# Attention, a mixture of experts and a soft mixture on one core: work on h's operands a step later, weight differences and dispatch at other places

## The chip, the cores and the metric

The kernel runs on one core of a Trainium2 chip. The metric is the device time of one execution in microseconds, the median of a few runs. TensorE multiplies matrices; its output goes to PSUM banks, which VectorE (DVE in the profile) and ScalarE (ACT) must empty before a bank can be used again. SyncE (SP) issues nearly all DMA transfers. GpSimd (POOL) has next to nothing to do.

## The reference

Three stages follow each other, for 2304 tokens of width 512:

```python
kv  = einsum('bhsd,bhse->bhde', k, v)            # attention, 4 batches of 576 tokens, 8 heads of 64
out = einsum('bhsd,bhde->bhse', q, kv)
x   = out / sqrt(mean(out*out, -1) + 1e-6) * g_norm
# mixture of experts, dense: every token goes through all 4 experts
for e in range(4):
    h = maximum(x @ w1[e], 0)                    # 512 -> 1024
    y += p[:, e:e+1] * (h @ w2[e])               # 1024 -> 512
# soft mixture: 8 experts x 4 slots, on y
logits = y @ phi                                 # 2304 x 32
d = exp(logits - logits.max(0)); d /= d.sum(0) + 1e-9     # dispatch: softmax over the tokens
slots = d.T @ y                                  # then a small two-layer network for each expert
c = softmax over the slots of logits
result = c @ slot_out
```

## The kernel before

**Tiles and chunks.** The 2304 tokens are 18 tiles of 128. Chunks 0 to 3 hold four tiles each, chunk 4 two. The first mixture goes through the chunks in two groups: group 0 is chunks 0 and 1, with experts 0, 1, 2, 3; group 1 is chunks 2, 3 and 4, with experts 3, 2, 1, 0. Expert 3 is thus used by both groups one after the other, and its weights stay in SBUF (it is the one called KEPT); those of experts 0 to 2 are prepared for group 0, stored to DRAM and read back for group 1.

**Products.** For accuracy each f32 operand is split into two f16 numbers, a high and a low half, and a product takes three f16 matmuls. The high half is a conversion on ScalarE (for weights L607, for h L821 and L823), the low half is the difference of the number and its high half, on VectorE (L609, L828, L832); the low half therefore waits for the high one. "First product" means h = relu(x w1), "second product" means h w2 with the addition to the output, scaled by p. Both are done for most chunks with seven block products in place of eight (numbered P 1 to 7), for which sums and differences of blocks of x, of h and of the weights are needed: S1 to S4 of h, T1 to T4 of a weight. In a first product TensorE writes to p (L913), and `fast_h` (L810) empties it with copies on ScalarE (L845, L847, L849, L863) and additions on VectorE (L851, L855, L859) and makes the operands of h. In a second product TensorE writes to m (L1012), and L1026 on ScalarE and L1028 on VectorE add m into the output; the second products of expert 3 for chunk 0, and of some others, take another form (y, L976, L987).

**The main list.** All of this is a list of 548 steps of TensorE's work, written out in order; a usual step takes 1.31 us, one of chunk 4's first product about half. Expert 3 runs through all chunks from step 180 to 314:

| steps | what | begins at, us |
|---|---|---|
| 180 to 193, 194 to 209 | chunk 0, first and second product | 281.4, 305.45 |
| 210 to 223 | chunk 1, first product | 328.82 |
| 224 to 237 | chunk 2, first product (group 1 begins) | 360.47 |
| 238 to 251 | chunk 1, second product | 385.58 |
| 252 to 265 | chunk 3, first product | 410.30 |
| 266 to 279 | chunk 2, second product | 437.31 |
| 280 to 293 | chunk 4, first product | 456.53 |
| 294 to 307, 308 to 314 | chunks 3 and 4, second product | 465.91, 484.25 |
| from 315 | expert 2 with group 1 | 493.42 |

**Background work.** Everything else is cut into small steps and strewn between the main ones: the preparing of weights, the attention of the next chunks (with its products kv, L278, o, L333, and xT, L402), and the dispatch softmax of finished chunks (`disp_steps`). `chain(start, stop, steps, ...)` (L1329) spreads such a list evenly from main step start to main step stop; `run_bg` takes from each chain what is due. So the place of an instruction in an engine's order follows from the marks given to its chain. An engine works through its order strictly; an instruction that waits holds up all behind it. `pe(f)` defers a background step's TensorE part until the main step's matmuls are issued.

The chains that the change touches: `prep_t2(e)` (L714) makes the differences T1 to T4 of expert e's w2 for group 1: in two halves four subtractions on VectorE (L727), four high parts on ScalarE (L607) and four low parts on VectorE (L609), and for e = 0 to 2 two stores each to DRAM. `kv_steps(3)` and `attn_steps([3])` are the attention of batch and chunk 3; kv's two banks are copied to kvs on VectorE (L302). `disp_steps(c)` computes chunk c's logits (lg, L1068), their maximum (L1088, L1092), the exponential dT (L1107, on ScalarE), its transpose dtr on TensorE (L1115) with the copy d (L1131), the product sp with its sum sacc (L1150), and the softmax over the slots (L1168 to L1186). ScalarE loads a table (ACT_TABLE_LOAD) when it passes between the square root of the attention (L377) and an exponential.

**Tasks on h.** The work on h's operands that isn't done at once is put in a queue, `todo`, as small tasks; `work_off(n, c, op)` (L804) takes n of them at each main step, and all up to the one for operand (c, op) before a product needs that:

```python
while todo and (n > 0 or any(o == (c, op) for o, _ in todo)):
    todo.popleft()[1]()
    n -= 1
```

**Loads.** SBUF is 47 pages of 4 KB in each partition, and PSUM eight banks. `want` puts loads in one list, and `pump` issues them in that order on SyncE's queue when pages are free, leaving as many free as the running chains claim. The read-backs of an expert's operands ("o1", "o2") stand at the end of the list, and the list halts at them until the main step gate[e]:

```python
key = loads[0][0]
if key[0] in ("o1", "o2") and now < gate[key[1]]:
    return
load_next()
```

## Time and profile before

| | us |
|---|---|
| median of 3 runs | 841.62 (841.59 to 842.0) |
| the profiled execution | 840.22 |
| its span, first to last instruction | 838.3 |
| TensorE busy | 806.4 (96%) |
| VectorE busy | 565.5 (67%) |
| ScalarE busy | 371.4 (44%) |

TensorE's granted clock was 0.997 of full speed in the mean. The busy shares are means over stages with different limits: in some stages VectorE has as much to do as TensorE, in others half of it. A row "[2.19 <-ACT pages L863]" says that the engine was idle for 2.19 us before this instruction, and that an instruction of ScalarE at line 863 that writes pages ended it.

### The profile page before, as it was taken

Reading aid. Unit: us, or ns where it says so; the run is one execution under the profiler, and the core shown is the slowest. Engines: PE = TensorE matmul, PEld = TensorE weight load, DVE = VectorE, ACT = ScalarE, POOL = GpSimd, SP = SyncE. Lnnn points to the kernel's source line nnn. Section 1 sums busy time; section 2 is a strip of 40 time slices with the busy share of each in tenths; the row PEclk is TensorE's granted clock in tenths of the full one; section 3 lists DMA queues with packets and bytes.
Section 4 is the critical chain, followed back from the end, with each engine's and each line's share of the span. In section 5 each row is a group of like instructions: output and inputs, shape, how many; then the busy total and the mean of one; then the engine's idle time right before and its main releaser. Section 6 shows DMA issues by size and latency. Waiting matters only on the chain.

```text
span 838.3 us, 17438 instructions
## 1 busy us (share of the span) xinstructions
PE 806.4 (96%) x7409; PEld 630.8 (75%) x7409; DVE 565.5 (67%) x1106; ACT 371.4 (44%) x735; POOL 13.1 (2%) x16
## 2 busy tenths in 40 slices
PE   7989999999999999889799999999999999999996
PEld 6865748575766676678689988898889888984444
DVE  7889978956895567778887426875488638742403
ACT  2684565653556145664565435240454125421202
POOL 4000000000000000000000000000000000000000
PEclk9999999999999999999999999999999999999998
DMA  8950700294239632100112350042202262669697
GB/s 331 387 216 26 248 4 21 91 380 188 76 102 405 247 114 113 51 27 1 51 52 74 105 180 23 1 177 98 105 2 93 89 223 76 214 235 355 197 402 232
DMA packets 40910, 126.01 MB, mean 150 GB/s; under 512 B 4224, under 2 KB 11264, under 8 KB 40832
## 3 DMA queue, kind: packets, MB, share of 16 engines
q1 hardware_dynamic: 40384, 124.80, 40.5%
q8 instruction: 58, 0.95, 0.5%
q14 instruction: 20, 0.16, 0.1%
q10 hardware_dynamic: 448, 0.10, 0.1%
HBM read 96.57 MB, written 28.31 MB: 149 GB/s over the span
## 4 chain that ended last, share of the span: by engine, by line
PE 80%; DVE 12%; ACT 5%; issue 1%; DMA 1%; ACTq 0%; DVEq 0%
PE p L913 31%; PE m L1012 20%; PE y L976 19%; PE s L1657 2%; PE so L1687 2%; PE kv L278 1%; PE o L333 1%; DVE mx_w L535 1%; DVE pages L930 1%; DVE pages L476 1%; DVE t L943 1%; DVE pages L609 1%; ACT pages L821 1%; DMA gT<-in_g 1%; PE x2T L1045 1%
## 5 line engine op out<-in xcount | busy, mean ns | idle before, releaser
L913 PE MATMUL p<-pages 128*128 128x256 f16 (+1 forms) x3360 | 340.9, 262 | 1.5 <-DVE pages L476 0.5
L913 PEld LDWEIGHTS <-pages 128*128 128x128 f16 x3360 | 299.9, 98 | 37.2 <-issue 5.1
L1012 PE MATMUL m<-pages 128*128 128x256 f16 x1680 | 186.5, 273 | 4.2 <-DVE pages L1028 4.2
L1012 PEld LDWEIGHTS <-pages 128*128 128x128 f16 x1680 | 164.1, 98 | 23.7 <-issue 4.9
L976 PE MATMUL y<-pages 128*128 128x512 f16 x768 | 170.9, 379 | 1.2 <-DVE pages L930 1.1
L976 PEld LDWEIGHTS <-pages 128*128 128x128 f16 x768 | 74.7, 98 | 87.0 <-DVE pages L930 1.6
L1028 DVE SCALAR_TENSOR_TENSOR pages<-m,pc,pages 128x256 f32<-128x256 f32 x120 | 53.6, 480 | 59.2 <-PE m L1012 59.0
L607 ACT ACTIVATE pages<-pages,s_w 128x512 f16<-128x512 f32 (+1 forms) x113 | 77.9, 739 | 32.3 <-DVE s_w L585 11.6
L609 DVE SCALAR_TENSOR_TENSOR pages<-pages,s_w 128x512 f16<-128x512 f32 (+1 forms) x113 | 83.9, 778 | 3.6 <-ACT pages L607 3.5
L823 ACT CAST pages<-t 128x512 f16<-128x512 f32 (+1 forms) x72 | 39.1, 549 | 65.8 <-DVE t L866 33.1
L929 ACT ACTIVATE pages<-t 128x512 f16<-128x512 f32 x48 | 30.0, 628 | 39.3 <-DVE t L943 38.9
L821 ACT ACTIVATE pages<-pages 128x512 f16<-128x512 f32 (+1 forms) x48 | 26.8, 558 | 46.1 <-DVE pages L855 24.5
L938 ACT COPY t<-p 128x512 f32<-128x512 f32 x48 | 27.1, 582 | 43.7 <-PE p L913 43.7
L943 DVE TENSOR_TENSOR t<-p,t 128x512 f32<-128x512 f32 x48 | 32.7, 686 | 17.2 <-PE p L913 17.1
L832 DVE TENSOR_TENSOR pages<-t,pages 128x512 f16<-128x512 f32 (+1 forms) x72 | 42.4, 596 | 2.3 <-ACT pages L823 0.9
L828 DVE SCALAR_TENSOR_TENSOR pages<-pages 128x512 f16<-128x512 f32 (+1 forms) x48 | 28.6, 599 | 15.4 <-ACT pages L821 15.0
L930 DVE SCALAR_TENSOR_TENSOR pages<-t,pages 128x512 f16<-128x512 f32 x48 | 32.8, 683 | 8.6 <-ACT pages L929 7.9
L987 DVE SCALAR_TENSOR_TENSOR pages<-y,pc,pages 128x512 f32<-128x512 f32 x24 | 18.0, 749 | 26.1 <-PE y L976 26.1
L823 ACT CAST pages<-pages 128x512 f16<-128x512 f32 (+1 forms) x24 | 13.0, 550 | 37.8 <-DVE t L870 37.8
L851 DVE TENSOR_TENSOR t<-p,t 128x512 f32<-128x512 f32 (+1 forms) x24 | 14.4, 598 | 19.4 <-PE p L913 16.6
L845 ACT COPY t<-p 128x512 f32<-128x512 f32 (+1 forms) x24 | 11.8, 515 | 31.2 <-PE p L913 31.1
L855 DVE TENSOR_TENSOR pages<-p,pages 128x512 f32<-128x512 f32 (+1 forms) x24 | 14.3, 598 | 16.4 <-PE p L913 14.8
(179 smaller groups left out, 705.3 us busy)
## 6 DMA issues: line engine op xcount, KB each, us to landing
pages<-in_w SPq DMA_DIRECT2D x48, 512.0 KB, 7.9
o<-pages SPq DMA_DIRECT2D x33, 512.0 KB, 9.8
pages<-o SPq DMA_DIRECT2D x33, 512.0 KB, 4.8
pages<-in_m SPq DMA_DIRECT2D x32, 512.0 KB, 5.2
pages<-in_m2a SPq DMA_DIRECT2D x16, 512.0 KB, 4.7
pages<-in_m2b SPq DMA_DIRECT2D x16, 512.0 KB, 10.3
o_t<-pages SPq DMA_DIRECT2D x12, 512.0 KB, 2.6
pages<-o_t SPq DMA_DIRECT2D x12, 512.0 KB, 4.5
```

Of the source, the lines that this page charges most:

```text
L607: nc.scalar.activation(dst[:, 0], src, AF.Copy, scale=s)
L609: nc.vector.scalar_tensor_tensor(out=dst[:, 1], in0=src, scalar=s, in1=dst[:, 0], op0=ALU.mult, op1=ALU.subtract)
L821: nc.scalar.activation(dst, sh(src), AF.Relu)
L823: nc.scalar.copy(dst, sh(src))
L832: nc.vector.tensor_tensor(out=h[:, 1], in0=sh(src), in1=h[:, 0], op=ALU.subtract)
L913: nc.tensor.matmul(ps[:, fp * n:fp * n + n], l, r, start=(fp + i == 0 and P in first), stop=(fp == 1 and i == len(mms) - 1 and P in end), ...
L929: nc.scalar.activation(hh, src, AF.Relu)
L930: late.append(lambda: nc.vector.scalar_tensor_tensor(out=hl, in0=src, scalar=0.0, in1=hh, op0=ALU.max, op1=ALU.subtract))
L943: nc.vector.tensor_tensor(out=t, in0=ps, in1=t, op=ALU.add)
L976: nc.tensor.matmul(ps, a, b, start=(u + kk + fp + i == 0), stop=(u == 1 and kk == 1 and fp == 1 and i == 2))
L1012: nc.tensor.matmul(ps, l, r, start=(i == 0 and j == 0 and P in (1, 2, 7)), stop=(i == len(mms) - 1 and j == nh - 1 and P in (2, 3, 4)), sk ...
L1028: nc.vector.scalar_tensor_tensor(out=x, in0=src, scalar=pc, in1=x, op0=ALU.mult, op1=ALU.add)
```

## The change

There are five edits.

1. A task that is put in `todo` may be taken not by the next call of `work_off` but from the one after it on: `turn` counts the calls, and each task carries its number. What a product needs is still taken ahead of that product.
2. Expert 2's `prep_t2` moves from steps 182 to 206 to steps 280 to 307 (from chunk 4's first product on). Its raw loads move behind the loads of q 6 to 8 and wait for step 274.
3. Expert 3's `prep_t2` moves from steps 208 to 225 to steps 194 to 223.
4. Dispatch of chunk 0 is spread over steps 210 to 237 in place of 210 to 223, that of chunk 1 over 255 to 279 in place of 252 to 265.
5. The attention of chunk 3 begins at step 222 in place of 224.

```diff
@@ pump
-            if key[0] in ("o1", "o2") and now < gate[key[1]]:
+            if now < gate.get(key[1] if key[0] in ("o1", "o2") else key[:3], now):
                 return
@@ the list of loads
-    want_t(E - 2)
     want_t(E - 1)
     want_kv(7)
     want_kv(8)
     for i in range(6, 9):
         want(("q", i), qT[i], 4)
+    want_t(E - 2)
@@ work_off
+        turn[0] += 1
-        while todo and (n > 0 or any(o == (c, op) for o, _ in todo)):
+        while todo and (n > 0 and todo[0][2] < turn[0] or any(o == (c, op) for o, _, _ in todo)):
             todo.popleft()[1]()
@@ fast_h
-            todo.append(((c, op), f))
+            todo.append(((c, op), f, turn[0] + 1))
@@ the chains
-    chain(m["mm1", 1, E - 1, 2], m["mm1", 1, E - 1, 3], kv_steps(3) + attn_steps([3], V), 6, 1.0)
+    chain(m["mm1", 1, E - 1, 2] - 2, m["mm1", 1, E - 1, 3], kv_steps(3) + attn_steps([3], V), 6, 1.0)
-    chain(m["mm1", 0, E - 1, 1], m["mm1", 1, E - 1, 2], disp_steps(0), 2, 1.0)
-    chain(m["end", 0, E - 1, 1], m["mm2", 1, E - 1, 2], disp_steps(1), 2, 1.0)
+    chain(m["mm1", 0, E - 1, 1], m["mm2", 0, E - 1, 1], disp_steps(0), 2, 1.0)
+    chain(m["end", 0, E - 1, 1] + 3, m["end", 1, E - 1, 2], disp_steps(1), 2, 1.0)
     for e in FAST:
-        chain(m["mm1", 0, e + 1, 0] + 2, m["mm1", 0, e + 1, 1] - (0 if e < E - 2 else 4), prep_t2(e, V), 4)
+        if e < E - 2:
+            chain(m["mm1", 0, e + 1, 0] + 2, m["mm1", 0, e + 1, 1], prep_t2(e, V), 4)
+        else:
+            chain(m["mm1", 1, E - 1, 4], m["mm2", 1, E - 1, 4], prep_t2(e, V), 4)
+            gate["w2", 1, e] = m["mm1", 1, E - 1, 4] - 6
         gate[e] = m["mm1", 1, e + 1, 3]
-    chain(m["mm1", 0, E - 1, 1] - 2, m["mm1", 1, E - 1, 2] + 2, prep_t2(E - 1, V), 4)
+    chain(m["mm2", 0, E - 1, 0], m["mm1", 1, E - 1, 2], prep_t2(E - 1, V), 4)
```

The lines of the new kernel have numbers two higher behind L806 (L828 is L830, L1028 is L1030, L913 is L915).

The orders below show three places. In the names, t_0_3_1_1 is the temporary of chunk 1's first product with expert 3, second half; p_0_3_2_0 and p_0_3_2_1 are the banks of chunk 2's first product; s_w_3 and s_w_2 are the scales of expert 3's and expert 2's weights; kv_3706 and kv_3605 are kv of batch 3.

First place: VectorE where chunk 2's first product begins (step 224), before:

```order
L609 SCALAR_TENSOR_TENSOR pages<-pages,s_w_3_2800 128x512
L832 TENSOR_TENSOR pages<-t_0_3_1_0_3382,pages 128x512
L609 SCALAR_TENSOR_TENSOR pages<-pages,s_w_3_2800 128x512
L832 TENSOR_TENSOR pages<-t_0_3_1_1_3406,pages 128x512
L851 TENSOR_TENSOR t_0_3_2_0_3730<-p_0_3_2_0_3770,t_0_3_2_0_3730 128x512
L870 SCALAR_TENSOR_TENSOR pages<-pages 128x512
L851 TENSOR_TENSOR t_0_3_2_1_3757<-p_0_3_2_1_3796,t_0_3_2_1_3757 128x512
L870 SCALAR_TENSOR_TENSOR pages<-pages 128x512
L302 COPY kvs<-kv_3706 64x4x64 x2
```

and now:

```order
L868 SCALAR_TENSOR_TENSOR t_0_3_1_0_3359<-t_0_3_1_0_3359,pages 128x512
L868 SCALAR_TENSOR_TENSOR t_0_3_1_1_3375<-t_0_3_1_1_3375,pages 128x512
L1170 TENSOR_REDUCE mc_3689<-ltr_3630 128x4
L1172 TENSOR_TENSOR ce_3691<-ltr_3630,mc_3689 128x128
L834 TENSOR_TENSOR pages<-t_0_3_1_0_3359,pages 128x512
L302 COPY kvs<-kv_3605 64x4x64 x2
L853 TENSOR_TENSOR t_0_3_2_0_3685<-p_0_3_2_0_3725,t_0_3_2_0_3685 128x512
L834 TENSOR_TENSOR pages<-t_0_3_1_1_3375,pages 128x512
```

Expert 3's low parts are gone from here, dispatch 0's softmax over the slots has come, and the copies of kv stand ahead of chunk 2's first additions rather than behind them. On TensorE the matmul that follows the last kv has, in the new order, a wait that the old one has not:

```order
L915 MATMUL p_0_3_2_0_3672<-pages 128x256
L278 MATMUL kv_3605<-pages 64x64 x10
L915 LDWEIGHTS pages [waits DVE_49]
L915 MATMUL p_0_3_2_1_3703<-pages 128x256 [waits PE_49]
L915 LDWEIGHTS pages
```

The wait is for VectorE's copies of kv, whose bank p_0_3_2_1 takes over.

Second place: VectorE in chunk 4's first product (steps 280 to 293), before:

```order
L832 TENSOR_TENSOR pages<-t_0_3_3_0_4289,pages 128x512
L832 TENSOR_TENSOR pages<-t_0_3_3_1_4313,pages 128x512
L851 TENSOR_TENSOR t_0_3_4_0_4844<-p_0_3_4_0_4862,t_0_3_4_0_4844 128x256
L828 SCALAR_TENSOR_TENSOR pages<-t_0_3_4_0_4844,pages 128x256
L851 TENSOR_TENSOR t_0_3_4_1_4860<-p_0_3_4_1_4878,t_0_3_4_1_4860 128x256
L828 SCALAR_TENSOR_TENSOR pages<-t_0_3_4_1_4860,pages 128x256
L855 TENSOR_TENSOR pages<-p_0_3_4_0_4831,pages 128x256
L828 SCALAR_TENSOR_TENSOR pages<-pages 128x256
```

and now:

```order
L834 TENSOR_TENSOR pages<-t_0_3_3_1_4268,pages 128x512
L727 TENSOR_TENSOR pages<-pages 128x2x256 x2
L853 TENSOR_TENSOR t_0_3_4_0_4808<-p_0_3_4_0_4828,t_0_3_4_0_4808 128x256
L727 TENSOR_TENSOR pages<-pages 128x2x256
L853 TENSOR_TENSOR t_0_3_4_1_4825<-p_0_3_4_1_4844,t_0_3_4_1_4825 128x256
L830 SCALAR_TENSOR_TENSOR pages<-t_0_3_4_0_4808,pages 128x256
L727 TENSOR_TENSOR pages<-pages 128x2x256
L830 SCALAR_TENSOR_TENSOR pages<-t_0_3_4_1_4825,pages 128x256
L609 SCALAR_TENSOR_TENSOR pages<-pages,s_w_2_2016 128x512 x2
L857 TENSOR_TENSOR pages<-p_0_3_4_0_4795,pages 128x256
L609 SCALAR_TENSOR_TENSOR pages<-pages,s_w_2_2016 128x512
L857 TENSOR_TENSOR pages<-p_0_3_4_1_4812,pages 128x256
```

Expert 2's subtractions and low parts have come between the additions, and a low half of h (L830) no longer stands right behind the addition it belongs to.

Third place: ScalarE where dispatch 1's exponential dT is computed, before:

```order
L847 COPY pages<-p_0_3_3_1_4300 128x512
L849 COPY pages<-p_0_3_3_0_4444 128x512
L377 ACTIVATE rms_4326<-rms_4326 128x16
L1107 ACT_TABLE_LOAD
L1107 ACTIVATE dT_4464,sm_4465<-LT_92,neg_4437 128x128
```

and now:

```order
L1028 ACTIVATE pages<-m_0_3_2_4510,pc_2805 128x256 x2
L408 COPY pages<-xT_4617 128x512
L1109 ACT_TABLE_LOAD
L1109 ACTIVATE dT_4639,sm_4640<-LT_92,neg_4572 128x128
L1111 ACTIVATE al_4577<-al_4577 128x1
```

It has moved from chunk 3's first product, where it stood among the copies from p, to chunk 2's second product, where it stands behind the emptying of m.

## Rows read from the trace of the kernel before

**Rows 1.** The page: TensorE's busy time, share and instructions

```profile
PE 806.4 (96%) x7409; PEld 630.8 (75%) x7409; DVE 565.5 (67%) x1106; ACT 371.4 (44%) x735; POOL 13.1 (2%) x16
```

**Rows 2.** TensorE's timeline, 318 to 496 us, all with idle time ahead (start, duration)

```profile
340.22 1.06 PE L1068 MATMUL lg<-pages,phiT 128*32 128x128 f32 x26 [0.40 <-ACT pages L1057]
...
350.63 0.33 PE L1115 MATMUL dtr<-ident,dT 128*128 128x128 f32 x1 [3.64 <-ACT dT L1107]
...
359.59 0.95 PE L278 MATMUL kv<-pages 64*64 64x64 f32 x20 [2.19 <-ACT pages L863]
...
395.45 2.78 PE L1012 MATMUL m<-pages 128*128 128x256 f16 x24 [0.98 <-DVE pages L1028]
...
400.71 5.40 PE L1012 MATMUL m<-pages 128*128 128x256 f16 x48 [1.60 <-DVE pages L1028]
...
407.69 2.78 PE L1012 MATMUL m<-pages 128*128 128x256 f16 x24 [1.58 <-DVE pages L1028]
...
413.89 0.44 PE L1045 MATMUL x2T<-ident,pages 128*128 128x128 f32 x2 [1.90 <-DVE pages L1028]
```

**Rows 3.** Busy time by stage: PE, PEld, DVE, ACT, POOL (instructions), clock, DMA

```profile
328.82:360.47 31.65, 25.39 (x257) 20.88 (x255) 24.15 (x47) 19.86 (x42) 0.00 (x0) 1.00 0.12 39
...
385.58:410.30 24.72, 20.56 (x186) 18.16 (x184) 23.56 (x53) 10.94 (x23) 0.00 (x0) 1.00 0.07 23
...
456.53:465.91 9.38, 9.38 (x171) 9.38 (x169) 5.48 (x13) 4.94 (x14) 0.00 (x0) 1.00 0.63 222
465.91:484.25 18.34, 18.34 (x172) 16.44 (x170) 9.44 (x25) 6.40 (x18) 0.00 (x0) 1.00 0.19 61
```

**Rows 4.** The page's costliest groups: h's low halves (busy, mean, idle before)

```profile
L828 DVE SCALAR_TENSOR_TENSOR pages<-pages 128x512 f16<-128x512 f32 (+1 forms) x48 | 28.6, 599 | 15.4 <-ACT pages L821 15.0
```

**Rows 5.** Timeline of all engines, 345 to 352 us: the first exponential

```profile
347.63 0.63 ACT L821 ACTIVATE pages<-pages 128x512 f16<-128x512 f32 x1 [2.64 <-DVE pages L855]
...
348.29 0.69 DVE L828 SCALAR_TENSOR_TENSOR pages<-pages 128x512 f16<-128x512 f32 x1 [0.70 <-ACT pages L821]
348.78 1.28 ACT L1107 ACT_TABLE_LOAD   x1
...
350.08 0.40 ACT L1107 ACTIVATE dT<-LT,neg 128x128 f32<-128x128 f32 x1
```

**Rows 6.** Groups of 283 to 330 us: expert 2's differences (busy, mean ns, idle)

```profile
L727 DVE TENSOR_TENSOR pages<-pages 128x512 f32<-128x512 f32 x10 | 6.9, 686 | 0.1
L609 DVE SCALAR_TENSOR_TENSOR pages<-pages,s_w 128x512 f16<-128x512 f32 x8 | 5.9, 746 | 2.4 <-ACT pages L607 2.4
...
L607 ACT ACTIVATE pages<-pages,s_w 128x512 f16<-128x512 f32 x8 | 5.5, 715 | 0.0
```

**Rows 7.** The page's DMA issues: KB each, us to landing

```profile
pages<-in_w SPq DMA_DIRECT2D x48, 512.0 KB, 7.9
...
pages<-o SPq DMA_DIRECT2D x33, 512.0 KB, 4.8
```

**Rows 8.** VectorE's timeline, 352 to 362 us: two instructions of dispatch 0

```profile
353.99 0.29 DVE L1186 TENSOR_TENSOR ce<-ce,sc 128x128 f32<-128x128 f32 x1
...
360.04 0.68 DVE L1150 COPY sacc<-sp 128x512 f32<-128x512 f32 x1
```

**Rows 9.** Timelines of ScalarE and VectorE: ahead of kv, and its copies

```profile
357.51 0.63 ACT L821 ACTIVATE pages<-pages 128x512 f16<-128x512 f32 x1 [0.83 <-DVE pages L859]
...
358.96 0.57 ACT L863 ACTIVATE pages<-p 128x512 f32<-128x512 f32 x1
...
370.15 0.85 DVE L302 COPY kvs<-kv 64x256 f32<-64x256 f32 x2
```

**Rows 10.** VectorE's timeline, chunk 1's second product: one of the evictions

```profile
402.38 0.87 DVE L1028 SCALAR_TENSOR_TENSOR pages<-m,pc,pages 128x256 f32<-128x256 f32 x2
```

**Rows 11.** ScalarE's timeline: a copy of xT, the second table load, a pair L1026

```profile
390.15 0.59 ACT L408 COPY pages<-xT 128x512 f32<-128x512 f32 x1 [0.94 <-PE xT L402]
...
427.54 1.28 ACT L1107 ACT_TABLE_LOAD   x1
...
457.47 0.83 ACT L1026 ACTIVATE pages<-m,pc 128x256 f32<-128x256 f32 x2
```

More of the change, by code (lines that the diff above doesn't have):

```diff
@@ L782, in attn_moe_softmoe_kernel @@
     todo = deque()
+    turn = [0]
     def hset(wk, c):
```

## The prediction

> **What bounds the kernel now.** I read the page's first lines, then the list of TensorE's stretches with what ended each idle time, then busy time by stage. TensorE works 806.4 of 838.3 us [rows 1], so nothing but a wait of TensorE, or work for it, can move the time. From step 180, where expert 3's run begins, to step 315, where it ends, the stretch that the change touches, it waits seven times [rows 2]: 0.40, 3.64, 2.19, 0.98, 1.60, 1.58 and 1.90 us, together 12.29 us. The full-speed clock held in all these windows [rows 3], so these waits are the whole pool from which the change can gain.
>
> They stand in two places. The first is chunk 1's first product with expert 3 (steps 210 to 223, 328.8 to 360.5): VectorE is busy 24.15 us there and TensorE 25.39 of 31.65 us. The second is chunk 1's second product (238 to 251, 385.6 to 410.3): VectorE 23.56 us, TensorE 20.56 of 24.72 [rows 3]. In the second VectorE is plainly the longer, and all of TensorE's waits name its evictions L1028. In the first nothing is longer than TensorE; there VectorE and ScalarE stand behind each other. VectorE's low half (L828) waits for ScalarE's high half (L821) right ahead of it, 15.0 us over 48 instructions of the whole run [rows 4]; while it waits, whatever else is queued on VectorE waits too. One such round: the high half 2.64 us late (347.63), VectorE's low half waiting 0.70 us for it (348.29), and only then ScalarE's table load (348.78, 1.28 us) and the exponential dT (350.08) whose transpose TensorE awaits [rows 5].
>
> **The change part by part.**
>
> *Work taken up a step later.* The number of instructions is the same. A low half now comes at least a step (1.31 us, from 18.34 us over 14 steps, [rows 3]) behind its high half (0.63 us, [rows 5]), and other work stands between. This removes VectorE's stalls of 0.70 us each [rows 5], of which TensorE sees only what the seven waits hold. Its cost: each product's operands are ready one or two steps later. Before a product needs its operand, the code forces what is due, so the order stays sound; I cost this at nothing, since no product among steps 252 to 315 waited for an operand [rows 2], and at one low half (0.69 us) a product if that cover fails.
>
> *Expert 2's differences, to steps 280 to 307.* 8 subtractions at 0.686 and 8 low parts at 0.746 us are 11.5 us of VectorE, 8 high parts at 0.715 us are 5.7 us of ScalarE [rows 6]. They leave the stages from 288 to 320 us, where TensorE doesn't wait, so that by itself gains nothing; it makes room there for expert 3's differences. Their four raw loads (7.9 us to landing, [rows 7]) are put behind step 274 and ahead of the read-backs on SyncE's queue. The first two take pages whose last use is at step 260, the others at 278, two steps ahead of 456.5: landed by 462 at the latest, and first used behind step 294 (465.9), two by two. The first operand read back is needed at step 315, the stored differences at 343, some 40 steps behind the last low part: hidden, and without that cover one load, 4.8 us [rows 7].
>
> *Expert 3's differences, to steps 194 to 223.* Between the first addition of chunk 1 and that of chunk 2, VectorE's list held 8 low parts and 4 subtractions of it, and now holds 4 low parts: 4 x 0.746 + 4 x 0.686 = 5.7 us less of 24.15.
>
> *Dispatch 0 spread to step 237.* Eight VectorE instructions of it leave too, L1150 (0.68) and seven of up to 0.29 us (as L1186), some 2.3 us [rows 8]. So VectorE has about 24.15 - 5.7 - 2.3 = 16 us in steps 210 to 223, against TensorE's 25, of which dispatch's own products also leave. The lg wait 0.40 goes. The dT transpose, 3.64 us: the copy ahead (0.6, as [rows 9]), the load and dT are 2.3 us on ScalarE, and TensorE comes to the transpose some four steps, 5 us, after the maximum; I take 0, and 3.64 as the other end. Late next is kv3.
>
> *kv3.* It starts two steps earlier and takes another PSUM bank, psO, which chunk 2's first product needs right behind: the second half's weight load waits for VectorE (the order below), for two copies L302. Before, TensorE waited 2.19 us ahead of kv [rows 2], for ScalarE's L863 behind L821 [rows 9]. That is gone; instead it waits for the copies, 0.85 us [rows 9], plus the hand-over: 1.0 us, from 0.85 (VectorE level) to 2.2 us (VectorE as late as before, the old wait).
>
> *Chunk 1's second product.* Of VectorE's 53 instructions there one reduction and one difference leave and one low half comes, each some 0.6 us as L828 [rows 4]: about 23 us against TensorE's 20.56, still 2.4 us more. The queue comes into the stage less late, which covers a little: I walked the evictions L1028 (0.87 us a pair, two steps to do it in, [rows 10]) through the new order and get 0.2 us at step 246 and 1.75 at step 250, together 2.0 in place of 0.98 + 1.60 + 1.58 = 4.16. Ends: 0 and 4.16. The x2T transposes, which paid 1.90 us for the same evictions, stand three steps later, behind other work: 0, at most 1.9.
>
> *Dispatch 1 to steps 255 to 279.* The transpose now comes two second-product steps (2 x 1.31 = 2.62 us) behind its maximum. ScalarE has to do a scaling pair L1026 (0.83), a copy L408 (0.59), the table load (1.28) and dT (0.40): 3.1 us, so 0.5 us late, with the hand-over 0.6. ScalarE's rows are [rows 11]. Ends: 0, as the same load at 427.54 delayed nothing [rows 2, 11], and 3.64, the old wait for it. The table is loaded as often as before. The exponential starts 1.30 us behind the start of a load of 1.28 us, so the load is the whole price [rows 5]. The Trainium skill (ScalarE: Activation LUTs, What ACT_TABLE_LOAD costs) adds a drain of about 1380 ns to the load; here no such gap shows. By that page this step would wait 2.0 instead of 0.6 us.
>
> *Chunk 4's first product (280 to 293).* It lasts 9.38 us, with VectorE busy 5.48 [rows 3]. 4 subtractions and 4 low parts add 4 x 0.686 + 4 x 0.746 = 5.7, a difference L832, about as long as L828's 0.6 [rows 4], leaves: 10.6 us, 1.2 more than the product lasts, and four high parts of 0.715 us stand between the copies that empty TensorE's banks. I take 1.4 us. Low end 0.5 (the excess drains into the next product, 18.34 us, with VectorE's 9.44 plus 5.7); high end 9.7, four low parts each waiting 2.4 us, what all eight together waited for L607 before [rows 6].
>
> **The sum.** Gone: 12.3. New: 1.0 + 2.0 + 0.6 + 1.4 = 5.0. The profiled execution took 840.22 us (838.3 of span and 1.9 around it); less 7.3 that is 832.9. The median of the runs is 841.62, 1.4 above the profiled one, so the forecast is 834.3 us. What follows step 315 only shifts.
>
> **Rivals.**
> 1. *VectorE stays behind.* The waits move instead of going: kv 2.2, chunk 1's second product 4.16, x2T's 1.9 at the next product, dispatch 0.6, chunk 4's 1.4, together 10.3; gain 2.0, 839.6 us. For it: VectorE's work between 328 and 485 us even grows by 5.7 us or so, since expert 2's comes in. Against: it leaves just the stage of the first waits.
> 2. *All waits go.* 841.6 - 12.3 = 829.3; with VectorE's queue hiding the copies and chunk 4's excess. Against it: the new order itself makes TensorE's load wait for kvs, and 23 us against 20.6 don't fit.
> 3. *Slower: VectorE and ScalarE pass the turn in chunk 4's product.* Steps there last only 0.67 us (9.38 / 14), so a step's delay no longer covers a high part (0.72): each of the four low parts waits 2.4 us, 9.7 in all, and TensorE with them, since the additions that empty its banks stand behind them. With kv 2.2, 4.16 and dispatch 0.6 that is 16.7 against 12.3: 846.0 us. It decides from 5.3 us of waiting in chunk 4 on, all else at its high end. Against: subtractions and additions, which wait for no high part, now stand between the low parts.
> 4. *ScalarE pauses once more about the switch of tables*, for as long again as the load, 1.28 us [rows 5]: dispatch 1's transpose waits 0.6 + 1.3 = 1.9, the time is 835.6 us. Against it: nothing lies between a load's end and its exponential [rows 5]. This is the drain that the Trainium skill's page above states; with its figure it would be 835.7.
> 5. *The delay of a step doesn't keep the halves apart*, because what is due is forced: then L828's stalls stay while the moves still count; this is rival 1 by another cause, and its time.
>
> **How the numbers follow.** Forecast 0.72; rivals 1 and 5 together 0.15; 2, 0.05; 3, 0.05; 4, 0.03. A measurement of this kernel tells 0.2%, 1.7 us, from no change. Half of rivals 1 and 5 lies within that (above 839.9), and 0.01 of the forecast: faster 0.87, same 0.08, slower 0.05. The single costs at their low ends (0.85, 0, 0, 0.5) give 841.6 - 12.3 + 1.35 = 830.7; the upper end holds rival 1 up to its middle, 839.6 and a little: range 830.5 to 840.
>
> **What would show it.** Right: no wait of TensorE above 0.5 us from step 210 to 224; in chunk 1's second product waits of 1.5 to 2.5 us, on L1030 (the old L1028); one of about 1 us behind kv3's products, on the copies L302; about 0.6 at the second dT transpose; 1 to 2 in chunk 4's first product; L830 (the old L828) waiting a few us in all instead of 15. Wrong: waits of over 4 us in either place that was relieved, or over 5 us in chunk 4's product, or a read-back for step 315 that comes late, which I put at nothing.

## The result, and the profile after

The changed kernel takes 831.01 us (median of 4 runs, 830.16 to 832.02) against 841.61 us before, measured beside it: a ratio of 0.9874, with a 95% interval of 0.9857 to 0.9891, or 10.6 us less. The forecast was 834.3 us in a range of 830.5 to 840: the direction and the range hold, and the gain is larger than the 7.3 us of the sum.

TensorE's timeline of the changed kernel from 280 to 500 us, all rows with idle time ahead (start, duration, and in brackets the idle time and what ended it), is the counterpart of [rows 2]:

```profile
358.63 4.11 PE L915 MATMUL p<-pages 128*128 128x256 f16 x36 [0.96 <-DVE kvs L302]
...
393.89 5.40 PE L1014 MATMUL m<-pages 128*128 128x256 f16 x48 [0.69 <-DVE pages L1030]
...
400.87 2.78 PE L1014 MATMUL m<-pages 128*128 128x256 f16 x24 [1.58 <-DVE pages L1030]
...
438.69 0.33 PE L1117 MATMUL dtr<-ident,dT 128*128 128x128 f32 x1 [0.59 <-ACT dT L1109]
...
457.14 0.83 PE L915 MATMUL p<-pages 128*128 128x128 f16 x12 [0.17 <-DVE pages L857]
```

The seven waits of 12.29 us have become five of 3.99 us. No wait is left between steps 210 and 224, and x2T no longer waits. Chunk 1's second product keeps two of its three waits on the evictions (0.69 and 1.58), and three are new: the copies of kv, the second dT, and chunk 4's first product. By stage (PE, PEld, DVE, ACT, POOL busy with instructions, then the granted clock, DMA share and GB/s), as in [rows 3]: chunk 1's first product, its second product, chunk 4's first product, chunk 3's second product:

```profile
330.19:355.31 25.12, 25.12 (x286) 21.90 (x285) 20.03 (x37) 17.11 (x37) 0.00 (x0) 1.00 0.16 45
...
380.80:403.48 22.68, 20.41 (x186) 18.17 (x184) 21.80 (x50) 8.99 (x18) 0.00 (x0) 1.00 0.01 2
...
447.93:457.81 9.88, 9.70 (x171) 9.46 (x169) 9.34 (x20) 7.25 (x19) 0.00 (x0) 1.00 0.42 124
457.81:476.15 18.34, 18.34 (x172) 16.44 (x170) 15.34 (x35) 9.30 (x22) 0.00 (x0) 1.00 0.80 301
```

Chunk 1's first product took 31.65 us and takes 25.12, all of it TensorE's; VectorE does 20.03 us of work there instead of 24.15. Chunk 4's takes 9.88 in place of 9.38, with VectorE busy for 9.34. The page's group of low halves, the counterpart of [rows 4]:

```profile
L830 DVE SCALAR_TENSOR_TENSOR pages<-pages 128x512 f16<-128x512 f32 (+1 forms) x48 | 27.6, 595 | 0.6 <-ACT pages L823 0.3
```

VectorE's 15.0 us behind the high halves, over the whole run, are down to 0.3.

From the first matmul of step 180 to that of step 315 TensorE took 212.03 us before (281.39 to 493.42) and takes 202.57 (282.75 to 485.32): 9.46 us less. In these two stretches the sums over the stages are, before,

```profile
sum 212.03, PE 199.66 PEld 166.39 DVE 150.34 ACT 107.37 POOL 0.95; mean PE 22.18 PEld 18.49 DVE 16.70 ACT 11.93 POOL 0.11
```

and after

```profile
sum 202.57, PE 198.56 PEld 166.58 DVE 149.68 ACT 107.56 POOL 0.95; mean PE 22.06 PEld 18.51 DVE 16.63 ACT 11.95 POOL 0.11
```

The idle time fell from 12.37 to 4.01 us (8.36), and the same matmuls also count 1.10 us less as busy. Another 0.55 us comes later, in steps of 0.19 us or less. The start, before any edit, took 1.36 us longer in this profiled execution than in the one before: the last section shows it to be the clock, nearly all of it. One of the five executions of the kernel with edits 1 and 4 took 1109.88 us at a mean clock of 0.752; every figure of that kernel below is from the other four.

### The profile page after: what moved, and what is told of

Its sections match the earlier page's. It is cut to its first block, busy times and chain, and to the rows that moved or that the text cites. A ratio compares the mean times of both kernels' runs of the same rounds, so it can differ in the third digit from the quotient of the medians.

```text
span 829.5 us, 17455 instructions
## 1 busy us (share of the span) xinstructions
PE 807.1 (97%) x7409; PEld 633.1 (76%) x7409; DVE 564.8 (68%) x1106; ACT 372.7 (45%) x735; POOL 13.1 (2%) x16
## 4 chain that ended last, share of the span: by engine, by line
PE 86%; DVE 9%; ACT 2%; issue 1%; DMA 1%; ACTq 0%; DVEq 0%
PE p L915 35%; PE m L1014 20%; PE y L978 19%; PE s L1663 2%; PE so L1693 2%; PE kv L278 2%; PE o L333 2%; DVE mx_w L535 1%; PE x2T L1047 1%; PE lg L1070 1%; DVE pages L609 1%; PE xT L402 1%; DVE t L945 1%; DMA gT<-in_g 1%; PE f L1726 1%
## 5 line engine op out<-in xcount | busy, mean ns | idle before, releaser
L915 PE MATMUL p<-pages 128*128 128x256 f16 (+1 forms) x3360 | 339.9, 262 | 2.6 <-DVE kvs L302 1.0
L915 PEld LDWEIGHTS <-pages 128*128 128x128 f16 x3360 | 300.0, 98 | 37.1 <-issue 3.8
L1030 DVE SCALAR_TENSOR_TENSOR pages<-m,pc,pages 128x256 f32<-128x256 f32 x120 | 53.6, 479 | 54.3 <-PE m L1014 53.9
L857 DVE TENSOR_TENSOR pages<-p,pages 128x512 f32<-128x512 f32 (+1 forms) x24 | 14.4, 601 | 25.5 <-PE p L915 25.4
L830 DVE SCALAR_TENSOR_TENSOR pages<-pages 128x512 f16<-128x512 f32 (+1 forms) x48 | 27.6, 595 | 0.6 <-ACT pages L823 0.3
```

The source lines that it names most:

```text
L830: nc.vector.scalar_tensor_tensor(out=h[:, 1], in0=sh(src), scalar=0.0, in1=h[:, 0], op0=ALU.max, op1=ALU.subtract)
L915: nc.tensor.matmul(ps[:, fp * n:fp * n + n], l, r, start=(fp + i == 0 and P in first), stop=(fp == 1 and i == len(mms) - 1 and P in end), ...
L1030: nc.vector.scalar_tensor_tensor(out=x, in0=src, scalar=pc, in1=x, op0=ALU.mult, op1=ALU.add)
```

## The experiments

All times were measured beside runs of the kernel before (medians 841.87 to 842.05 us in the four groups of runs; 841.61 beside the changed kernel), and the ratios are to those. "Stretch" is TensorE's time from step 180 to step 315 in the profiled execution. The waits are the idle times that TensorE's timeline names there: D, dispatch 0 (lg, ltr or dT's transpose); K, kv or its copies; S, chunk 1's second product; X, x2T; D2, dispatch 1 (with its ltr and sp); C, chunk 4's first product and chunk 3's second.

| kernel | us | ratio (95%) | stretch | D | K | S | X | D2 | C |
|---|---|---|---|---|---|---|---|---|---|
| before | 841.61 | 1 | 212.03 | 4.04 | 2.19 | 4.16 | 1.90 | 0 | 0 |
| edit 1 alone | 839.25 | 0.9975 (0.9965 to 0.9985) | 210.35 | 3.64 | 0 | 4.19 | 1.90 | 0 | 0 |
| edits 2, 3 alone | 842.89 | 1.0018 (1.0008 to 1.0028) | 215.83 | 3.07 | 0.28 | 4.38 | 1.90 | 0 | 2.80 |
| edit 4 alone | 840.94 | 0.9989 (0.9981 to 0.9998) | 211.55 | 6.07 | 0 | 4.03 | 0 | 0.59 | 0 |
| edits 1, 4 | 835.46 | 0.9923 (0.991 to 0.9937) | 206.21 | 2.53 | 0 | 4.19 | 0 | 0.59 | 0 |
| all but edit 1 | 839.29 | 0.9973 (0.9963 to 0.9984) | 209.84 | 2.46 | 0.96 | 2.12 | 0 | 0.59 | 2.81 |
| all but edit 5 | 833.6 | 0.9902 (0.9889 to 0.9916) | 204.73 | 0.63 | 0 | 4.18 | 0 | 0.59 | 0.16 |
| changed | 831.01 | 0.9874 (0.9857 to 0.9891) | 202.57 | 0 | 0.96 | 2.27 | 0 | 0.59 | 0.17 |
| + kv's bank | 830.45 | 0.9862 (0.9849 to 0.9875) | 201.66 | 0 | 0 | 2.28 | 0 | 0.60 | 0.46 |
| + kv's bank, tasks rest | 829.07 | 0.9853 (0.9831 to 0.9875) | 200.71 | 0 | 0 | 0 | 0 | 0.59 | 1.40 |

In the first three kernels with edits alone, and in all but edit 1, the stretch also holds a fall of TensorE's clock (last section), so it moves by other amounts than the waits; what an edit is worth is therefore taken from the ratios. Edits 2 and 3 were run only together.

### Each edit by itself

**Edit 1 alone.** The diff is that of `work_off` and `fast_h` alone, of which the lines in `work_off`:

```diff
-        while todo and (n > 0 or any(o == (c, op) for o, _ in todo)):
+        turn[0] += 1
+        while todo and (n > 0 and todo[0][2] < turn[0] or any(o == (c, op) for o, _, _ in todo)):
```

> The kernel before with edit 1 alone (tasks on h taken up a step later). Theory A, load: VectorE has as much to do as TensorE in steps 210 to 223 and more in 238 to 251, and edit 1 takes none of it away; it only ends the stalls between high and low half. So the 3.64 us ahead of dT's transpose shrinks by a part (it is behind one late high half), kv's 2.19 and the 4.16 of chunk 1's second product stay by and large: 838 to 840 us, a gain of 2 to 4. Theory B, stalls: the 15 us that VectorE stood behind ScalarE's high halves are what made it late; then edit 1 alone brings most of the gain, 835 us or less.

839.25 us, within theory A's range, but by other waits than it names. VectorE's stalls behind the high halves are gone (0.3 us of 15.0 are left), lg's and kv's waits too; dT's transpose still waits 3.64 us, to the hundredth what it waited before. TensorE's timeline of this kernel, two of the rows, and the row of ScalarE's ahead of dT's table load:

```profile
350.75 0.33 PE L1117 MATMUL dtr<-ident,dT 128*128 128x128 f32 x1 [3.64 <-ACT dT L1109]
...
413.67 0.44 PE L1047 MATMUL x2T<-ident,pages 128*128 128x128 f32 x2 [1.90 <-DVE pages L1030]
```

```profile
347.75 0.63 ACT L823 ACTIVATE pages<-pages 128x512 f16<-128x512 f32 x1 [2.64 <-DVE pages L857]
```

ScalarE is idle for the same 2.64 us as in [rows 5], and the table load and dT stand behind this conversion in its order. What it waits for is an addition (L857) that has eleven other instructions ahead of it in VectorE's order, worked through from 342.86 to 347.72 all but without a gap. So the 0.70 us of [rows 5] was not what made this dT late: VectorE's queue ahead of the addition was, and the place of dT behind the conversion.

**All but edit 1.** The changed kernel with edit 1 taken back, here and in `work_off`:

```diff
-            todo.append(((c, op), f, turn[0] + 1))
+            todo.append(((c, op), f))
```

> The changed kernel with edit 1 undone: all moves, but tasks on h taken up at the next call as before. Theory A, load: the waits in steps 210 to 223 go by the moves alone; L828 (here with the new line numbers) again stands behind its high half in chunk 4's first product, where expert 2's differences now are, and TensorE waits 2 to 4 us there: 833 to 836 us. Theory B, stalls: the moves do little without edit 1: 838 us or more.

839.29 us: theory A had 833 to 836 and falls, theory B's 838 or more holds; by the ratios edit 1 is worth 8.3 us once the moves are there, and 2.1 by itself (0.0025 of 842). The wait of dispatch 0 isn't gone by the moves: it stands at ltr, 2.46 us, for the copy LT. In chunk 4's first product, the low halves are again right behind their high halves. VectorE's timeline there:

```profile
455.11 0.41 DVE L851 TENSOR_TENSOR t<-p,t 128x256 f32<-128x256 f32 x1
456.01 0.43 DVE L828 SCALAR_TENSOR_TENSOR pages<-t,pages 128x256 f16<-128x256 f32 x1 [0.48 <-ACT pages L821]
456.35 0.69 DVE L727 TENSOR_TENSOR pages<-pages 128x512 f32<-128x512 f32 x1
456.95 0.42 DVE L851 TENSOR_TENSOR t<-p,t 128x256 f32<-128x256 f32 x1
457.86 0.43 DVE L828 SCALAR_TENSOR_TENSOR pages<-t,pages 128x256 f16<-128x256 f32 x1 [0.48 <-ACT pages L821]
```

and that of the changed kernel at the same place:

```profile
451.13 0.42 DVE L853 TENSOR_TENSOR t<-p,t 128x256 f32<-128x256 f32 x1
451.47 0.68 DVE L727 TENSOR_TENSOR pages<-pages 128x512 f32<-128x512 f32 x1
452.07 0.42 DVE L853 TENSOR_TENSOR t<-p,t 128x256 f32<-128x256 f32 x1
452.40 0.41 DVE L830 SCALAR_TENSOR_TENSOR pages<-t,pages 128x256 f16<-128x256 f32 x1
```

The work is the same; with edit 1 there is no hole in it. TensorE's waits in chunk 4's product and the one behind it are 2.81 us without edit 1, and 0.17 with it.

**Edits 2 and 3 alone.** The lines of the diff on loads and on `prep_t2`, of which the chains:

```diff
+            chain(m["mm1", 1, E - 1, 4], m["mm2", 1, E - 1, 4], prep_t2(e, V), 4)
-    chain(m["mm1", 0, E - 1, 1] - 2, m["mm1", 1, E - 1, 2] + 2, prep_t2(E - 1, V), 4)
+    chain(m["mm2", 0, E - 1, 0], m["mm1", 1, E - 1, 2], prep_t2(E - 1, V), 4)
```

> The kernel before with edits 2 and 3 alone (w2 differences of experts 2 and 3 moved). Theory A: VectorE is 5.7 us lighter in steps 210 to 223, so lg's 0.40 and most of dT's 3.64 go, kv's 2.19 and the 4.16 plus 1.90 stay; chunk 4's first product gets 2 to 3 us of new waits as the low halves still stand behind their high halves: 838 to 841 us. Theory B: dT's transpose waits for a chain on ScalarE and stays late; with the new waits the time is 841.6 to 845.

842.89 us, 1.0008 to 1.0028 times before: the differences' moves are a small loss by themselves. Here theory B was right on dT's transpose: VectorE has 20.52 us of work in steps 210 to 223 in place of 24.15, 3.6 less and not 5.7, and the transpose still waits 3.07 us. What the moves cost at chunk 4 (2.80 us) is what theory A said.

**Edit 4 alone.**

```diff
-    chain(m["mm1", 0, E - 1, 1], m["mm1", 1, E - 1, 2], disp_steps(0), 2, 1.0)
-    chain(m["end", 0, E - 1, 1], m["mm2", 1, E - 1, 2], disp_steps(1), 2, 1.0)
+    chain(m["mm1", 0, E - 1, 1], m["mm2", 0, E - 1, 1], disp_steps(0), 2, 1.0)
+    chain(m["end", 0, E - 1, 1] + 3, m["end", 1, E - 1, 2], disp_steps(1), 2, 1.0)
```

> The kernel before with edit 4 alone (dispatch of chunks 0 and 1 spread out). Theory A: dT's transpose has four steps more, so its 3.64 go, and lg's 0.40; x2T's 1.90 go as they stand three steps later; at the second dT 0.6 comes; kv's and the 4.16 stay: a gain of about 5, 836 to 838 us. Theory B: VectorE and ScalarE are late anyway, dispatch's instructions come into chunk 2's first product and make the evictions there late: a gain under 2 us.

840.94 us: the gain is under 2 us, as theory B says. x2T's 1.90 go, and dT's 3.64 go as theory A says, but dispatch 0 now waits 6.07 us one instruction earlier, at ltr, which neither theory has:

```profile
357.43 0.48 PE L1160 MATMUL ltr<-ident,LT 128*128 128x128 f32 x1 [6.07 <-ACT LT L1078]
```

ScalarE's timeline ahead of it in this kernel, and one of VectorE's rows there:

```profile
347.90 0.63 ACT L821 ACTIVATE pages<-pages 128x512 f16<-128x512 f32 x1 [1.62 <-DVE pages L855]
348.44 0.60 ACT L474 CAST pages<-pages 128x512 f16<-128x512 f32 x1
350.50 0.63 ACT L821 ACTIVATE pages<-pages 128x512 f16<-128x512 f32 x1 [1.45 <-DVE pages L855]
353.09 0.63 ACT L821 ACTIVATE pages<-pages 128x512 f16<-128x512 f32 x1 [1.96 <-DVE pages L859]
...
355.68 0.63 ACT L821 ACTIVATE pages<-pages 128x512 f16<-128x512 f32 x1 [0.83 <-DVE pages L859]
...
357.13 0.24 ACT L1078 COPY LT<-lg 128x128 f32<-128x128 f32 x1
```

```profile
348.57 0.69 DVE L828 SCALAR_TENSOR_TENSOR pages<-pages 128x512 f16<-128x512 f32 x1 [0.70 <-ACT pages L821]
```

This is what the wait at ltr hangs on. ScalarE is idle for 5.86 us of these ten, four times behind an addition of VectorE; VectorE in turn stands 0.69 or 0.70 us behind each of the four high halves. The two engines pass the turn to each other, each with its queue behind it, and LT, a copy of 0.24 us whose input lg was done at 348.63, comes last. Edit 1 lets VectorE go on to the next addition; what it takes off this wait, the next run shows.

### Which edits belong together

**Edits 1 and 4**, the two diffs of these edits above on the kernel before.

> The kernel before with edits 1 and 4 alone. The single edits left a wait for dispatch 0 each: with edit 1 alone 3.64 us at dT's transpose, with edit 4 alone 6.07 us at ltr, behind ScalarE's copy LT. Theory C, ScalarE's queue and place together: only the two edits together take it away, as edit 4 puts the steps apart and edit 1 keeps ScalarE from standing behind VectorE; then lg, dT, kv and x2T are gone, 0.6 us at the second dT comes, chunk 1's second product keeps its 4.2: 834 us, plus or minus 0.7. Theory A, VectorE's load: without edits 2 and 3 the 5.7 us more of VectorE's work in steps 210 to 223 keep a wait of 2 us or more at ltr or dT: 836 us or more.

835.46 us (834.54 to 835.97), between the two theories' times. By the ratios the two edits are worth 6.5 us together, and 2.1 and 0.9 by themselves. TensorE's rows of dispatch 0:

```profile
353.94 0.33 PE L1162 MATMUL ltr<-ident,LT 128*128 128x128 f32 x1 [2.03 <-ACT LT L1080]
...
359.24 1.48 PE L915 MATMUL p<-pages 128*128 128x256 f16 x12 [0.50 <-DVE ce L1172]
```

With edit 1, LT comes at 353.64 in place of 357.13, and ltr waits 4.04 us less than with edit 4 alone. But 2.03 us are left, as theory A says, and 0.50 at ce (the softmax over the slots): theory C is right that both are needed, and wrong that they are enough. With the differences moved as well (all but edit 5) ltr's wait is 0.63, and the stretch another 1.5 us shorter.

**Edit 5 undone** (chunk 3's attention from step 224 again):

```diff
-    chain(m["mm1", 1, E - 1, 2] - 2, m["mm1", 1, E - 1, 3], kv_steps(3) + attn_steps([3], V), 6, 1.0)
+    chain(m["mm1", 1, E - 1, 2], m["mm1", 1, E - 1, 3], kv_steps(3) + attn_steps([3], V), 6, 1.0)
```

> The changed kernel with edit 5 undone: attention of chunk 3 begins at step 224 again. Theory C: the two steps earlier are what halved the waits in chunk 1's second product (2.27 against 4.16, which each of edits 1, 4 and 2 with 3 left at 3.9 or more), so they come back to about 4, and the 0.96 us for the copies of kv go with the other bank: 832 us. Rival: the w2 differences' leaving halved them; then only the 0.96 go, 830 us.

833.6 us, 2.6 above the changed kernel and 1.6 above theory C's time; the stretch is 2.16 longer. Theory C's cause holds: chunk 1's second product waits 1.00 + 1.60 + 1.58 = 4.18 us again, and the copies of kv don't wait. Edit 5 gains 1.9 there and 0.63 at ltr, and pays 0.96 for the bank; the other 0.6 of the 2.16 stand in no bracket.

### What is left

**kv of batch 3 in its own pool's bank** (run after the two that follow):

```diff
-                kv_ps[b] = ps_a(f"kv{b}")
+                kv_ps[b] = psA.tile([128, 512], F32, tag="a", name=f"kv{b}") if b == 3 else ps_a(f"kv{b}")
```

> The changed kernel with kv of batch 3 in the pool's own bank, nothing else. Theory: the 0.96 us for the copies of kv go and nothing comes in their place; the 0.59 at the second dT stays, but the 0.84, 0.25 and 0.19 that the run with the pause had at and before chunk 4's first product don't come: 830 us, 0.7 to 1 less than the changed kernel. Rival: VectorE, which sets chunk 1's second product, takes the 0.96 back there: 831 us.

830.45 us; in the profile the 0.96 us are gone, chunk 1's second product waits as before (0.70 and 1.58), and chunk 4's first now waits 0.46 for the copy cT, so it isn't so that nothing comes in their place. The stretch is 0.9 shorter. The intervals of the two ratios overlap, so the times alone do not tell the kernels apart.

**The bank, and a pause ahead of dispatch 1's transpose** (an empty background step in `disp_steps(1)`):

```diff
+        if c == 1:
+            st.insert(len(st) - 6, lambda: None)
```

> The changed kernel with kv of batch 3 always in a bank of its own pool (not the one that chunk 2's product takes over), and one empty background step between dispatch 1's exponential and its transpose. Theory C: the 0.96 us at kvs and the 0.59 us at the second dT go, what is saved isn't given back in chunk 1's second product: 829.5 us. Rival: TensorE comes to that product 1 us earlier, VectorE doesn't, so the waits there grow by as much; only 0.6 is gained: 830.5 us.

830.36 us (ratio 0.9864, 0.9849 to 0.9879): neither theory. The 0.96 and 0.59 go, but 0.19 (ltr), 0.25 (sp) and 0.84 (the copy cT, at chunk 4's first matmuls) come: the pause made the rest of dispatch 1 a step later, and its end now sits where steps last 0.67 us.

**Both of these, and chunk 3's attention from step 218** (four steps earlier than in the changed kernel):

```diff
-    chain(m["mm1", 1, E - 1, 2] - 2, m["mm1", 1, E - 1, 3], kv_steps(3) + attn_steps([3], V), 6, 1.0)
+    chain(m["mm1", 1, E - 1, 2] - 6, m["mm1", 1, E - 1, 3], kv_steps(3) + attn_steps([3], V), 6, 1.0)
```

> As the run with the bank and the pause, and attention of chunk 3 begins four steps earlier still (step 218). Theory C: VectorE and ScalarE have room in steps 210 to 223 (20 and 17 of 25 us), the same 30 background steps over 34 main steps take some 2 us of VectorE out of chunk 1's second product, whose waits fall from 2.3 to under 0.7: 828 us. Rival: VectorE comes late in steps 210 to 237 instead, new waits at chunk 2's first additions: 830.5 us or more.

831.82 us (0.9881, 0.9867 to 0.9894), the rival's side by the time, though its interval overlaps that of the run before. VectorE's work in chunk 1's second product falls by 0.4 us only, the waits there are 1.24 and 1.11, and a new one of 0.79, for ce, stands in chunk 2's first product.

**GpSimd computes the low parts of chunk 3's x** (with the bank):

```diff
+        low = nc.gpsimd if p[0] // 4 == 3 else eng
-            lambda: a_split(p, 0, 1, eng),
+            lambda: a_split(p, 0, 1, low),
...
```

> As the run with the bank, and GpSimd computes the low parts of chunk 3's attention output (L476, eight of VectorE's instructions, some 4.9 us, in chunk 1's second product). Theory: VectorE is what bounds that product (21.8 of 22.7 us), so without 4.9 us its waits on L1030, 2.3 us, go: 828 us. Rival: GpSimd, which takes 0.79 us for such a piece of half the size, slows VectorE as both work, or chunk 3's operands come late at step 252: 830 us or more.

833.75 us (0.9907, 0.9894 to 0.9921): a loss of 3.3 us against the bank alone. VectorE has 24.86 us of busy time in chunk 1's second product instead of 21.81, with 4.9 us of work taken away. VectorE's timeline there:

```profile
384.95 0.18 DVE L384 TENSOR_TENSOR rms<-rms 128x16 f32<-128x16 f32 x1
385.16 0.17 DVE L385 TENSOR_SCALAR rms<-rms 128x16 f32<-128x16 f32 x1
385.37 1.16 DVE L386 TENSOR_TENSOR rms<-rms 128x16 f32<-128x16 f32 x1
...
389.30 2.25 DVE L391 TENSOR_TENSOR pages<-pages,rms 128x512 f32<-128x512 f32 x2
391.47 1.64 DVE L832 SCALAR_TENSOR_TENSOR pages<-pages 128x512 f16<-128x512 f32 x1
```

and GpSimd's:

```profile
385.35 1.15 POOL L476 TENSOR_TENSOR pages<-pages 128x512 f16<-128x512 f32 x1 [333.42 <-DVE rms L385]
389.50 3.07 POOL L476 TENSOR_TENSOR pages<-pages 128x512 f16<-128x512 f32 x2 [3.00 <-ACT pages L474]
```

L386, some 0.17 us elsewhere, begins 0.02 us behind GpSimd's instruction and ends 0.03 us behind its end: VectorE stands still for the whole of this GpSimd instruction. The pair L391 takes 2.25 instead of 1.28 us. Not all of the loss is VectorE's: chunk 1's second product is 3.27 us longer than with the bank alone (25.96 against 22.69), and of that 1.67 us are 48 matmuls m that take 7.07 in place of 5.40 us at a lower clock behind a wait of 2.05 (last section).

**The same, with dispatch 1 a step earlier:**

```diff
-    chain(m["end", 0, E - 1, 1] + 3, m["end", 1, E - 1, 2], disp_steps(1), 2, 1.0)
+    chain(m["end", 0, E - 1, 1] + 2, m["end", 1, E - 1, 2] - 1, disp_steps(1), 2, 1.0)
```

> As the run with GpSimd, and dispatch 1 begins and ends one step earlier. Theory: the second dT's transpose then falls behind another step's emptying of m and its 0.59 us go: 0.5 us less than the run with GpSimd. Rival: the two steps between maximum and transpose stay two, so the wait only moves: no difference.

834.5 us (0.9917, 0.9903 to 0.993): no gain. The second dT doesn't wait now, but ltr does (0.20), and dispatch 1's products stand at other places.

**The bank, and four calls of `work_off` in chunk 1's second product that take no task:**

```diff
-        work_off(1, c, op)
+        calls[wk, c] = calls.get((wk, c), 0) + 1
+        work_off(0 if c == 1 and wk[1] == KEPT and 5 <= calls[wk, c] <= 8 else 1, c, op)
```

> As the run with the bank, and in chunk 1's second product four calls of work_off (steps 242 to 245) take no task unless the product needs it, so four of chunk 2's low halves and first sums (some 2.7 us of VectorE) move into chunk 3's first product, where VectorE has 17.8 of 21.9 us. Theory: VectorE's order, not another engine, holds chunk 1's second product by the 2.3 us that TensorE waits for L1030 there, so these go: 828.2 us. Rival: it was late already when the product began and the evictions stand behind what the product itself needs; then less than 1 us goes, or the waits come back at chunk 3's first additions: 830 us.

829.07 us (828.18 to 829.83), the lowest median of all; its ratio's interval overlaps those of the bank alone and of the changed kernel, so what follows is read from the profile. By stage, chunk 4's first product, chunk 1's second and chunk 3's first:

```profile
443.06:454.54 11.48, 10.09 (x170) 9.60 (x168) 11.48 (x24) 8.49 (x21) 0.00 (x0) 1.00 0.38 108
378.37:398.62 20.25, 20.24 (x187) 18.18 (x184) 19.38 (x46) 8.23 (x17) 0.00 (x0) 1.00 0.01 2
398.62:420.49 21.87, 21.87 (x202) 19.97 (x200) 17.74 (x35) 15.38 (x34) 0.95 (x1) 1.00 0.00 1
```

Chunk 1's second product has no wait left: 20.25 us in place of 22.69, with VectorE's work there down from 21.81 to 19.38. VectorE held it, as the theory says. 1.48 us of that are given back, not in chunk 3's additions as the rival has it but in chunk 4's first product, 11.48 in place of 10.00 us, where VectorE is now busy all the time; how the four tasks come to press there, two products later, was not followed up.

## Why the prediction came out as it did

**Right, with the sizes:** kv's copies (1.0, measured 0.96); the second dT (0.6, measured 0.59, with the load, copy and pair in ScalarE's order as priced), so no drain behind the table load, rival 4, came; x2T's wait gone by its later place (it stays at 1.90 with edit 1 and with edits 2 and 3 alone, and is 0 with edit 4 alone); the read-backs for step 315 hidden.

**Right in size, in part by luck:** chunk 1's second product (2.0, measured 2.27). VectorE had 21.80 us of work there and not 23, so the wait is not the excess of work that the prediction made it; what took the other 1.9 us away is edit 5, without which VectorE has 23.99 us of work there and 4.18 us of waiting are left. And the old 2.19 us ahead of kv went with edit 1 alone, with edit 4 alone and with edit 5 undone: the earlier start, which the prediction named, wasn't needed for it.

**Mis-sized, chunk 4's first product:** 1.4 us stood in the sum; the wait was 0.17, and the product took 0.50 us longer, the low end. I had counted 1.2 us of VectorE's work too much, plus a share for high parts between the copies. VectorE was busy 9.34 us there, not 10.6: one low part (at 458.00) ran on in chunk 3's second product, the mechanism of my low end, and I had added whole durations where neighbours overlap by 0.08 us. Rival 3's turn-passing in this place is real, but only without edit 1: 2.81 us there and in the product behind it.

**Mis-sized, the pool itself:** "these waits are the whole pool" missed 1.1 us that TensorE's rows count as busy. The end of a matmul is modelled in the profile, and the last one ahead of a wait counts 0.16 us more as busy than it does where the next instruction follows at once. The changed kernel's timeline has 48 matmuls m with nothing to wait for behind them:

```profile
385.61 5.40 PE L1014 MATMUL m<-pages 128*128 128x256 f16 x48
390.85 0.60 PE L402 MATMUL xT<-ident,pages 128*128 128x128 f32 x4
```

The next instruction begins 5.24 us behind their start. The 48 at 393.89 are followed by the wait of 1.58 and the next matmul at 400.87, 6.98 us behind: the pause is 1.74 and its bracket says 1.58. Before there were ten such places, three of them pauses too short for a bracket (ahead of ltr twice and of the second dT's transpose); after there are five. By that estimate 0.8 of the 1.1 us are pauses that stood in no bracket. With chunk 4's 1.2, less 0.3 at chunk 1's second product, this makes nearly all of the 2.16 us between the stretch's 9.46 and the 7.3 of the sum. The 0.55 us behind step 315 have no explanation from a run.

**A last step that didn't hold:** the sum made 832.9 for the profiled execution and added 1.4 us, by which the median before was above its profile. The changed kernel's profiled execution took 831.27, and its median of 831.01 is 0.3 below that. The 1.4 went with the clock (last section), and the prediction kept it for the changed kernel without a reason; half of the 3.3 us between forecast and measurement are this step.

**A term that was left out, though the number came out: dispatch 0.** The prediction took dT's 3.64 us away by four steps more for the transpose, and that held: no kernel with edit 4 has a wait there, and those without it have 3.64 (before, and with edit 1 alone) and 3.07 (with edits 2 and 3 alone). But the sum put the transpose ltr, one instruction earlier, at nothing, without a reason, and with edit 4 alone it waits 6.07 us. That it doesn't in the changed kernel takes all the rest: edit 1 (2.03 left, and 0.50 at ce), the moved differences (0.63 left), edit 5 (none). VectorE's work in steps 210 to 223, which the prediction had fall by 8.0 us to 16, fell by 4.1, and with all the moves but without edit 1 dispatch 0 still waits 2.46. So edit 1, which had no gain of its own in the sum, is what the others needed: by the ratios the edits gain 2.1 (edit 1), -1.5 (2 and 3) and 0.9 (4) by themselves, 1.5 us in all, and together with edit 5, which was not run alone, 10.6. The zero for dispatch 0 came true in part by luck.

## What to carry to other kernels

Where two engines hand each other halves of one operand, look at what else stands in their queues: the price of each hand-over (0.70 us here) is paid by instructions that have nothing to do with it, and a bystander's copy of 0.24 us made TensorE wait 6 us. Put other work between the halves before moving work about; the moves of the differences, which lost 0.2% by themselves, took 1.5 us off the stretch once edits 1 and 4 were there. And a wait that a move takes away should be looked for one instruction earlier and one stage later before it is booked as a gain.

## What the runs showed of the hardware

**The clock falls behind some waits.** The granted clock was 1.00 from 282 to 490 us in the profiles of before and after, but not in all: with edits 2 and 3 alone it fell behind x2T's wait of 1.90 us, which itself came right behind the waits of the second product. TensorE's timeline there:

```profile
412.40 0.44 PE L1045 MATMUL x2T<-ident,pages 128*128 128x128 f32 x2 [1.90 <-DVE pages L1028]
412.68 1.79 PE L913 MATMUL p<-pages 128*128 128x256 f16 x12
414.27 1.91 PE L333 MATMUL o<-kvs,pages 128*128 128x128 f32 x8
```

and the windows:

```profile
408.82:412.40 3.58, 1.69 (x16) 1.33 (x13) 3.19 (x7) 1.58 (x4) 0.00 (x0) 1.00 0.00 0
412.40:416.30 3.90, 3.90 (x24) 3.65 (x25) 1.54 (x3) 2.50 (x7) 0.00 (x0) 0.66 0.00 0
```

The eight matmuls o take 1.91 us; before, at the same place and behind the same wait of 1.90, they took 1.06. It was idle for half of 408.82 to 412.40. This fall to the lower level (1.2 of 2.4 GHz for a part of the window) cost 1.64 us (step 252 to 266 took 28.65 in place of 27.01). The same is to be seen behind ltr's 6.07 us with edit 4 alone (clock 0.87 from 355 to 381 us) and behind 2.05 us with GpSimd (0.93 from 381 to 404). With edit 1 alone it fell behind dT's 3.64 us (0.93 from 330 to 355), where it held at 1.00 before, behind a wait of the same length. A wait can thus cost more than its length, in some executions and not in others; the profile of before had no such fall in this stretch, and was 1.4 us under its median. Of 60 executions of that kernel beside the runs, the 11 with a mean clock of 0.994 or more took 839.83 to 841.00 us, and the 41 at 0.990 or 0.991 took 841.25 to 843.19.

**The start.** In the changed kernel's profile the clock stood at 0.50 from 14 to 19 us; in that of before, with the same code there, it was 1.00 (windows of the changed kernel, then of before):

```profile
14.00:19.00 5.00, 3.84 (x40) 3.54 (x41) 4.71 (x10) 2.20 (x3) 1.14 (x1) 0.50 1.03 399
```

```profile
14.00:19.00 5.00, 3.34 (x74) 3.02 (x70) 4.71 (x10) 2.18 (x3) 1.16 (x1) 1.00 1.03 399
```

40 matmuls ran in these 5 us in place of 74; it is nearly all of the 1.36 us by which the profiled execution was later at step 180 (0.11 of them were there at 13.5 us).

**VectorE and GpSimd.** VectorE's L386 stood still for the whole of GpSimd's L476 (1.16 us in place of 0.17). The Trainium skill (SBUF — State Buffer, SBUF: two separate sides) says that the two share a pair of ports as an exclusive lock held for the whole instruction, and that a VectorE instruction with two SBUF inputs is among those that need it. The rows agree: L386 has two, and began 0.02 us behind L476.
